# Block-sparse attention from the second batch on, with the drawn key blocks gathered by register offsets

## The chip, the cores and the metric

The kernel runs on one core of a Trainium2 chip. A core has five engines with instruction streams of their own: TensorE (PE, with its weight loads shown apart as PEld), VectorE (DVE), ScalarE (ACT), GpSimd (POOL) and SyncE (SP, which computes nothing and issues most DMAs here). They are tied together by semaphores, and each engine takes its instructions strictly in the order in which they were written. The metric is the device time of one execution in microseconds. Before the change it was 1061.06 us (median of 3 runs, 1060.33 to 1061.57).

## The reference

Attention over 4 batches, 8 heads, 768 positions of 64 numbers, with a block mask (24 blocks of 32), and then a Fourier mixing block with a two-layer channel network. All is float32.

```python
scores = scale * np.matmul(q, k.transpose(0, 1, 3, 2))
mask = np.abs(blk_i - blk_j) <= 1                       # neighbouring blocks
mask = mask | (blk_i == 0) | (blk_j == 0) | (blk_i == n_blocks - 1) | (blk_j == n_blocks - 1)
for qb in range(n_blocks):
    for kb in sampled_blocks[qb]:                       # three drawn blocks per query block
        mask[qb * block:(qb + 1) * block, kb * block:(kb + 1) * block] = True
scores = np.where(mask, scores, -1000000000.0)
attn = softmax(scores)                                  # max taken off, exp, divided by the sum + 1e-9
x = (attn @ v), heads side by side                      # (4, 768, 512)
mixed = np.real(np.fft.fft(np.fft.fft(x, axis=1), axis=2))
u = x + mixed
un = (u - mean(u)) / np.sqrt(var(u) + 1e-06)
return u + np.maximum(un @ w_ch1, 0.0) @ w_ch2          # 512 -> 2048 -> 512
```

A query block needs its own block, two neighbours, the first, the last and up to three drawn ones: at most 8 of 24. The queries of the first and the last block need every key. The drawn blocks are an input, known only when the kernel runs.

## The kernel before

**Pairs and units.** Two heads of one batch make a *pair*, 16 pairs in all (`pairs`, four to a batch). The two heads lie on the two halves of the 128 partitions. A pair has 12 *units* (`UP`): two halves of the queries (384 each) by six chunks of 128 keys. For a unit, `scores` (L560) makes 128 x 384 scores of each head in PSUM (L577, each head on its 64 rows of the array); `weigh` (L591) takes the exponential on ACT; `values` (L641) multiplies with v and adds into `o` over the six chunks (L651); `gather` (L618) adds the exponentials on POOL or DVE, for the sums of the softmax. All keys are computed, and the mask takes out what doesn't belong: either PE adds large negative numbers from two small factor tables (L587, while `masks["by_pe"]` holds), or DVE multiplies by a 0/1 mask after the exponential (L607; the mask is made in the first batch by `mask_step`, L367).

**Queries and keys.** For the first five pairs PE transposes q and k (`turn`, L495). From then on (`BY_VECTOR`) `load_blocks` (L221) loads 32x32 blocks with four transfers each for q and k, and DVE flips the blocks (`flip_blocks`). The queries stand in an order of their own (`_ORDER`) which the Fourier part wants; `in_order` copies q into it.

**Output.** When a half is done, `values` copies `o` to `oT` and `place` (PE) or `place_blocks` (L685: 16 transfers from SBUF to SBUF, issued on SP, in batches 2 and 3 for all but a batch's first pair) brings it into `x`, the tile of the batch. `x` has two buffers a half, so the third batch can be placed only when the first has left.

**The order of the work.** All instructions are in an order written out at build time. `slot` (L1379) takes two units at a time, 6 slots a pair, 24 a batch: scores of this slot, values of the one before, loads of later pairs, placing. Between, it puts the work of the batch before: the Fourier steps (`apart`) as gaps allow, and the channel products (`late`; `quad`, L1053 and `channels`, L1118) at a pace. The gaps come from a planner's own estimates of each engine's time (`when`, `busy`). At the first pair of the third and fourth batch, `until` (L1433, L1449) runs the channel products of the batch two back to the end as one block, since its `x` is needed. The channel weights are loaded and rounded beside the first batch's attention (`w_load`, `w_round`).

**Queues.** Nearly every DMA is issued on SP, in program order: q, k and v two pairs or one pair ahead, tables and weights in the first batch, `place_blocks`, the output. If SP has to wait for a buffer, everything behind it waits too.

Of the kernel before, what the change touches and what calls it, by code (L numbers as in the profile page):

```python
# [40 lines left out]
def _grid(ap, start, runs, jump, n, step):  # L41
# [25 lines left out]
_IN_ORDER = ((0, 0, (128, 128, 2), (64, 1, 2), (1, 2, 64)),  # L67
# [32 lines left out]
def kernel(  # L100
# [68 lines left out]
    mask = const.tile([P, C, S], U8, name="mask")  # L169
# [4 lines left out]
    ldv = ctx.enter_context(tc.tile_pool(name="ldv", bufs=2))  # L174
# [44 lines left out]
    BY_VECTOR = NP + 1  # L219

    def load_blocks(n, a, tile):  # L221


        b, j = pairs[n]
        for i in range(2):
            rows = (q, k)[a][b, 2 * j + i].rearrange("(t r) (g d) -> g r t d", r=BLK, d=BLK)
            for g in range(D // BLK):
                p0 = D * i + BLK * g
                nc.sync.dma_start(
                    out=tile[p0:p0 + BLK, :].rearrange("r (t d) -> r t d", d=BLK), in_=rows[g])  # L230
        loaded[n, a] = tile

    def load_k(n, queue=None, cuts=(slice(0, C),)):

        if n >= BY_VECTOR:
            load_blocks(n, 1, ld.tile([P, S], FP32, tag="k", name="kb"))
            return
# [11 lines left out]
    def load_q(n, ts=range(T)):  # L249

        if n >= BY_VECTOR:
            load_blocks(n, 0, ld.tile([P, S], FP32, tag="q", name="qb"))
            return
# [10 lines left out]
    def load_v(n, queue=None):  # L264

        b, j = pairs[n]
        vt = ldv.tile([P, 2, C, D], FP32, tag="v", name="vr")
# [3 lines left out]
        v_of[n] = vt  # L271

# [64 lines left out]
    factors = room(2, [P, 3, S], "factors", BF16)  # L337
    of_k, off_q, keep_q = (factors[:, i, :] for i in range(3))
# [3 lines left out]
    nc.vector.memset(keep_q, 0.0)  # L342

    def twice(t):
# [17 lines left out]
    keep = bit(NB)  # L362
    nc.vector.tensor_scalar(out=keep, in0=maskT, scalar1=0.0, scalar2=None,
                            op0=ALU.is_equal)
    spread_q(off_q[0:NB, :], maskT)
    twice(off_q)
    def mask_step(i):  # L367


        half, c = divmod(i, C)  # L370
        m, at = ps_m.tile([P, 512], FP32, tag="m", name="m"), bank("m")
        nc.tensor.matmul(m[:, 0:HS], of_k[0:D, c * P:(c + 1) * P],
                         keep_q[0:D, half * HS:(half + 1) * HS], start=True, stop=True)
        done = busy("PE", 0.17) + HOP

        def keep_it():
            nc.scalar.copy(out=mask[:, c, half * HS:(half + 1) * HS], in_=m[:, 0:HS])
            give(at, busy("ACT", 0.5, done))
        return keep_it
# [106 lines left out]
    by_pe, to_gather = set(), deque()  # L486
    masks = {"by_pe": True}

    turned, e_of, acc_of, o_of, sums_of, x_of, sp_of = {}, {}, {}, {}, {}, {}, {}
    s_at, e_at, e_free, oT_at, acc_at = {}, {}, {}, {}, {}  # L490
# [38 lines left out]
    def squares(n, a):  # L529

        t = loaded[n, a]
        if a == 0:
            turned[n, 0] = tp_p.tile([P, S], FP32, tag="qT", name="qT")
        nc.scalar.activation(out=t if a else turned[n, 0], in_=t, func=ACT.Square,
                             accum_out=peaks[:, 2 * n + a:2 * n + a + 1])
        busy("ACT", 1.05)

    def flip_blocks(n, a):
        t = loaded[n, a]
        out = t  # L540
        if a == 1:
            kT = turned[n, 1] = tp_p.tile([P, S], FP32, tag="kT", name="kT")
            out = _at(kT, 0, [(1, P), (P, C)])
        nc.vector.transpose(out=out, in_=t)
        busy("DVE", 1.0)

    def in_order(n):

        t = loaded[n, 0]
        qT = turned[n, 0]  # L550
        for to, frm, *dims in _IN_ORDER:
# [66 lines left out]
    def gather(u):  # L618
# [4 lines left out]
        if c == 0:  # L623
            return
# [1021 lines left out]
```

## Time and profile before

| what | value |
|---|---|
| median of 3 runs | 1061.06 us |
| the profiled execution | 1061.69 us, its span 1060.0 us |
| granted TensorE clock, mean | 0.994 |
| PE / DVE / ACT / POOL busy | 97% / 63% / 35% / 23% of the span |
| attention of pairs 0 to 3 (batch 0) | 7.8 to 126.8 us |
| pairs 4 to 7 (batch 1) | to 229 us |
| scores of pair 8, then the block of batch 0's channel products | to 248, to 410 us |
| pairs 9 to 11 with channel products between | to 537 us |
| pair 12, then a block of channel products | to 556, to 657 us |
| pairs 13 to 15 with channel products between | to 778 us |
| the rest: channel products, Fourier part and channel network of batch 3 | to 1060 us |

The page shows one profiled execution. Busy shares are of the span; a float32 product appears as two PE records, each with a weight load of its own. In a line of groups, `x768 | 154.8, 518 | 7.4` reads: 768 instructions, 154.8 us busy together, 518 ns one of them, 7.4 us idle of the engine just before them. `SPq` is SP issuing a DMA: the time stands for the issue, not for the transfer.

### The profile page before, as it was taken

How to read it: one execution, taken by the hardware profiler on the slowest of the kernel's cores; microseconds unless marked ns; L12 is line 12 of the kernel's file. 1: busy time of each engine (PE TensorE's matmuls, PEld its weight loads, DVE VectorE, ACT ScalarE, POOL GpSimd, SP SyncE). 2: the span in 40 equal slices, each digit the busy share in tenths (PEclk: the TensorE clock that was granted, in tenths of full speed). 3: DMA queues.
4: the chain of work that ended last, by engine and by line, in shares of the span. 5: the costliest groups of instructions: out<-in, count | busy, mean ns of one | idle time of the engine just before them, and what ended most of it. 6: DMA issues, size and time to landing. Idle time of an engine off the chain costs nothing.

```text
span 1060.0 us, 12495 instructions
## 1 busy us (share of the span) xinstructions
PE 1030.6 (97%) x4414; PEld 537.1 (51%) x4414; DVE 669.1 (63%) x1227; ACT 366.5 (35%) x736; POOL 240.5 (23%) x270
## 2 busy tenths in 40 slices
PE   8989999999999999999999999899999999999996
PEld 4333345445465454443534654354445564578585
DVE  6898795877746345655678364765447446774663
ACT  6978755564020122433441212343221111210210
POOL 1000183556000002554552001635420001000000
PEclk9999999999999999999999999999999999999998
DMA  7757522220000002231220001210000001000001
GB/s 217 229 166 222 112 46 45 45 46 15 1 1 0 1 1 57 52 56 27 41 54 0 1 1 44 63 33 19 8 15 0 1 0 42 19 1 1 0 18 46
DMA packets 120544, 46.27 MB, mean 44 GB/s; under 512 B 108172, under 2 KB 113562, under 8 KB 120474
## 3 DMA queue, kind: packets, MB, share of 16 engines
q1 hardware_dynamic: 119222, 44.66, 17.6%
q10 hardware_dynamic: 1220, 0.72, 0.3%
q8 instruction: 36, 0.59, 0.2%
q14 instruction: 34, 0.28, 0.1%
q0 software_dynamic: 32, 0.01, 0.0%
HBM read 36.72 MB, written 6.29 MB: 41 GB/s over the span
## 4 chain that ended last, share of the span: by engine, by line
PE 87%; DVE 6%; ACT 4%; issue 2%; DMA 1%; SPq 0%; POOL 0%; ACTq 0%; DVEq 0%; POOLq 0%
PE y L1122 23%; PE z L1066 16%; PE s L577 11%; PE o L651 10%; PE yp L1066 8%; PE yy L1187 7%; PE xp L1066 4%; PE zp L855 2%; PE s L587 1%; DVE t L1028 1%; ACT e L597 1%; PE sp L718 1%; PE sp L732 1%; PE utp L991 1%; PE xt L674 1%
## 5 line engine op out<-in xcount | busy, mean ns | idle before, releaser
L637 POOL TENSOR_TENSOR acc<-acc,e 128x384 f32<-128x384 f32 x158 | 160.9, 1052 | 87.1 <-DVE e L607 68.0
L577 PE MATMUL s<-qT,kT 64*128 64x384 f32 x768 | 154.8, 518 | 7.4 <-ACT e L597 5.8
L651 PE MATMUL o<-e,vr 128*64 128x384 f32 x768 | 143.1, 500 | 2.2 <-DVE oT L659 2.2
L1125 DVE TENSOR_TENSOR x<-y,x 128x512 f32<-128x512 f32 x72 | 49.8, 691 | 130.1 <-PE y L1122 129.8
L1122 PE MATMUL y<-w_sb,hB 128*128 128x512 f32 x288 | 128.0, 595 | 0.3 <-DVE x L1125 0.3
L1122 PE MATMUL y<-w_sb,hA 128*128 128x512 f32 x288 | 128.1, 594 | 0.0
L607 DVE TENSOR_TENSOR e<-s,mask 128x768 f32<-128x768 f32 x88 | 80.0, 950 | 48.9 <-ACT s L605 39.9
L577 PEld LDWEIGHTS s<-qT,kT 64*128 64x128 f32 x768 | 64.5, 187 | 85.7 <-ACT e L597 23.6
L605 ACT ACTIVATE s<-s 128x768 f32<-128x768 f32 x88 | 66.7, 792 | 92.6 <-PE s L577 92.4
L637 POOL TENSOR_TENSOR acc<-e 128x384 f32<-128x384 f32 x46 | 50.3, 1113 | 212.0 <-ACT e L597 125.9
L597 ACT ACTIVATE e<-s 128x768 f32<-128x768 f32 x104 | 79.1, 810 | 49.0 <-PE s L587 36.4
L1066 PE MATMUL z<-unT,t 128*128 128x384 f32 x256 | 93.4, 487 | 0.6 <-DVE hA L1071 0.6
L1122 PEld LDWEIGHTS y<-w_sb,hB 128*128 128x128 f32 x288 | 53.5, 190 | 65.5 <-issue 64.6
L1122 PEld LDWEIGHTS y<-w_sb,hA 128*128 128x128 f32 x288 | 53.6, 190 | 62.6 <-issue 59.9
L651 PEld LDWEIGHTS o<-e,vr 128*64 128x64 f32 x768 | 48.0, 136 | 72.7 <-issue 67.8
L1071 DVE TENSOR_TENSOR hA<-z,hA 128x384 f32<-128x384 f32 x64 | 35.7, 557 | 70.6 <-PE z L1066 70.6
L1075 ACT ACTIVATE hA<-hA 128x384 f32<-128x384 f32 x64 | 33.6, 524 | 122.5 <-DVE hA L1071 122.4
L1066 PEld LDWEIGHTS z<-unT,t 128*128 128x128 f32 x256 | 48.2, 190 | 35.6 <-DVE hA L1071 3.0
L1075 ACT ACTIVATE hB<-hB 128x384 f32<-128x384 f32 x64 | 33.6, 525 | 86.0 <-DVE hB L1071 86.0
L938 POOL TENSOR_SCALAR st<-st 128x1 f32<-128x1 f32 x24 | 8.3, 347 | 207.4 <-DVE st L937 207.3
L1086 ACT COPY hA<-xp 128x384 f32<-128x384 f32 x32 | 15.3, 479 | 111.6 <-PE xp L1066 111.6
L1066 PE MATMUL z<-t,w_sb 128*128 128x384 f32 x128 | 46.7, 488 | 0.7 <-DVE t L1028 0.7
(207 smaller groups left out, 1430.7 us busy)
## 6 DMA issues: line engine op xcount, KB each, us to landing
wraw<-in_moe_w_ch_dram SPq DMA_DIRECT2D x32, 512.0 KB
vr<-in_v_dram SPq DMA_DIRECT2D x30, 192.0 KB
qb<-in_q_dram SPq DMA_DIRECT2D x44, 96.0 KB
kb<-in_k_dram SPq DMA_DIRECT2D x44, 96.0 KB
x<-oT SPq DMA_DIRECT2D x192, 12.0 KB
out_dram<-x SPq DMA_DIRECT2D x11, 252.0 KB
out_dram<-x SPq DMA_DIRECT2D x18, 128.0 KB
qr<-in_q_dram SPq DMA_DIRECT2D x24, 64.0 KB
```

What stands on the lines that cost most here:

```text
L577: nc.tensor.matmul(s[:, i, 0:HS], kT[rows, c * P:(c + 1) * P], qT[rows, queries], start=True, stop=u not in by_pe)
L597: nc.scalar.activation(out=e, in_=s[:, :, 0:HS], func=ACT.Exp, scale=scale)
L605: nc.scalar.activation(out=s[:, :, 0:HS], in_=s[:, :, 0:HS], func=ACT.Exp, scale=scale)
L607: nc.vector.tensor_tensor(out=e, in0=s[:, :, 0:HS], in1=m.broadcast_to([P, 2, HS]), op=ALU.mult)
L637: nc.gpsimd.tensor_add(out=acc[:, i, :], in0=start[:, i, :], in1=e[:, i, :])
L651: nc.tensor.matmul(o[D * i:D * i + D, :], vt[:, i, c, :], e[:, i, :], start=(c == 0), stop=(c == C - 1))
L1066: nc.tensor.matmul(to, a[:, k, :], c[:, k, :], start=(k == 0), stop=(k == ND // 2 - 1))
L1071: tt(out=to, in0=ps, in1=a, op=ALU.add)
L1075: nc.scalar.activation(out=h, in_=h, func=ACT.Relu)
L1122: nc.tensor.matmul(y, hs[0, half][:, l, m * P:(m + 1) * P], w2_sb[:, 4 * r + l, :], start=(l == 0), stop=(l == 3))
L1125: nc.vector.tensor_tensor(out=x[:, m, :], in0=y, in1=x[:, m, :], op=ALU.add)
L1187: nc.tensor.matmul(ps, a[:, k, :], c[k // 2][:, k % 2, :] if isinstance(c, list) else c[:, k, :], start=(k == 0), stop=(k == 3))
```

## The change

For pairs 4 to 15 attention no longer computes all keys. A pair has 8 units in place of 12, in 4 slots (`KINDS`), and each half of the queries has four kinds:

- **E** and **O**: windows. The keys lie in eight chunks of three blocks (96 keys), with the first or the last block of all appended to each chunk by `copy_ends`, so that 128 keys meet the queries near them (`_WINDOWS`). Together they cover neighbours, the first and the last block. 352 query columns each; a table `near` of 0 and 1 takes out what doubles.
- **X**: drawn. For each of the 11 inner query blocks of the half, three drawn key blocks side by side (96 keys) meet 32 queries: 11 pieces. `gather_drawn` copies the key blocks on POOL from the flipped keys to `kr`, 33 copies of 32 columns at offsets read from a table into POOL's registers. `load_drawn` brings the same blocks of v from DRAM, 33 transfers on SP with an offset in a register. A table `drawn` takes out blocks that are drawn twice or are covered by a window.
- **G**: the queries of the first and the last block, against all keys: four chunks of 96 keys, 64 columns.

Score products are cut to 64 keys, so that one product covers a 64x64 part of the array. `kr` is one buffer for both halves. The drawn values lie in two tiles of the pool `ld`, which has one buffer for each name; both halves use the same two. q and k are loaded straight into the tiles that are flipped in place (k in 12 transfers a pair, before 4), v in chunks with the first and last block behind them (12 transfers a pair, before 2). The order of the queries is now made when `o` is copied out (`put`, small copies on ACT) and, for the sums, in `invert` (small copies on DVE). The tables are made once, in the first batch (`near_masks`, `drawn_load`, `drawn_masks`); `mask_step` and the mask are gone. Pair 4 is no longer transposed by PE.

Core of the diff:

```diff
-    BY_VECTOR = NP + 1
+    BY_VECTOR = NP
...
+                for x in range(CH):
+                    nc.sync.dma_start(
+                        out=tile[p0:p0 + BLK, :, BLK * x:BLK * x + BLK],
+                        in_=of.rearrange("(c x r) (g d) -> x g r c d", x=CH, r=BLK, d=BLK)[x, g])
...
+    def drawn_at(engine, row, most, m):
+        return nc.values_load_multi_w_load_instructions(
+            at_of[row:row + 1, NR * m:NR * min(m + 6, NQ)], engines=[engine], min_val=0, max_val=most,
+            skip_runtime_bounds_check_because="kept within the blocks by a minimum on the chip")[1]
...
+    def load_drawn(n, half):
+        b, j = pairs[n]
+        vr_of[n, half] = [ld.tile([P, 6, 2, D], FP32, tag=tag, name="vd") for tag in "qk"]
+        for m in range(NQ):
+            if m % 6 == 0:
+                at = drawn_at(mybir.EngineType.SP, 2 * BLK + BLK * half, S - BLK, m)
+            for r in range(NR):
+                nc.sync.dma_start(
+                    out=vr_of[n, half][m // 6][BLK * r:BLK * r + BLK, m % 6, :, :],
+                    in_=v[b, 2 * j:2 * j + 2, bass.ds(at[NR * (m % 6) + r], BLK), :].rearrange(
+                        "h s d -> s h d"))
+
+    def gather_drawn(n, half):
+        flat = turned[n, 1].rearrange("p c s -> p (c s)")
+        for m in range(NQ):
+            if m % 6 == 0:
+                at = drawn_at(mybir.EngineType.Pool, BLK * half, NCH * P - 2 * BLK, m)
+            for r in range(NR):
+                nc.gpsimd.tensor_copy(out=kr[:, m, BLK * r:BLK * r + BLK],
+                                      in_=flat[:, bass.ds(at[NR * (m % 6) + r], BLK)])
...
+    KINDS = ((0, "E"), (0, "O"), (0, "X"), (0, "G"), (1, "G"), (1, "E"), (1, "O"), (1, "X"))
...
+            for keys, to, of in parts:                      # few_scores
+                for i in range(2):
+                    for g in range(0, keys.shape[1], D):
+                        rows = slice(D * i, D * i + D)
+                        some = keys[rows, g:min(g + D, keys.shape[1])]
+                        nc.tensor.matmul(s[g:g + some.shape[1], i, to], some, of[rows],
+                                         start=True, stop=True)
...
+        elif kind == "X":                                   # few_values
+            rows = slice(0, NR * BLK)
+            parts = [(vr_of[n, half][m // 6][:, m % 6], to, to, False, True)
+                     for m, to, _ in pieces(half, kind)]
...
+        for vals, to, of, start, stop in parts:
+            for i in range(2):
+                nc.tensor.matmul(o[D * i:D * i + D, to], vals[rows, i, :], e[rows, i, of],
+                                 start=start, stop=stop, skip_group_check=True)
...
     def slot(sl):
...
+        if NP <= nxt < len(pairs):
+            if s == 0:
+                load_k(nxt)
+                load_q(nxt)
+            if s == (4 if not few else 2):
+                for a in (1, 0):
+                    squares(nxt, a)
+                    flip_blocks(nxt, a)
+                copy_ends(nxt)
+            if s == (5 if not few else 3):
+                gather_drawn(nxt, 0)
+            if s == 1:
+                load_chunks(nxt, 0)
+        if few and s == 1:
+            gather_drawn(n, 1)
+        if NP <= n < len(pairs) and s == 0:
+            load_chunks(n, 1)
+            load_drawn(n, 0)
+        if few and s == 2:
+            load_drawn(n, 1)
```

Scores of a slot come before the values of the slot before. So X of half 0 has its scores in slot 1 and its values in slot 2; X of half 1 has its scores in slot 3 and its values in slot 0 of the next pair.

More of the change, by code (lines that the diff above doesn't have):

```diff
@@ new lines, in gather_drawn @@
+    def gather_drawn(n, half):
[6 more added lines that the diff above has]
+                                      in_=flat[:, bass.ds(at[NR * (m % 6) + r], BLK)])
+                busy("POOL", 0.2)
+        kr_at[n, half] = when["POOL"] + HOP
@@ L538, in flip_blocks @@
     def flip_blocks(n, a):
[L539 to L544, printed above, removed]
-        busy("DVE", 1.0)
[L547 to L551, printed above, removed]
-            nc.scalar.copy(out=_at(qT, to, [(d[0], d[2]) for d in dims]),
-                           in_=_at(t, frm, [(d[1], d[2]) for d in dims]))
-        busy("ACT", 1.7, when["DVE"])
+        t = turned[n, a][:, :, 0:CH * BLK] if a else turned[n, 0]
@@ L556, with copy_ends @@
+        nc.vector.transpose(out=t, in_=t)
+        busy("DVE", 1.0)
+    def copy_ends(n):
+        kT = turned[n, 1]
+        last = CH * BLK
+        for odd, (c, x) in enumerate(((0, 0), (NCH - 1, CH - 1))):
+            src = kT[:, c, BLK * x:BLK * x + BLK].rearrange("p (o r) -> p o r", o=1)
+            nc.scalar.copy(out=kT[:, odd::2, last:last + BLK],
+                           in_=src.broadcast_to([P, NCH // 2, BLK]))
+        busy("ACT", 0.6, when["DVE"] + HOP)
     UP = 2 * C
-    UNITS = len(pairs) * UP
@@ L657, in values @@
             oT = sum_p.tile([P, HS], FP32, tag="oT", name="oT")
[L658 to L663 removed]
+            nc.scalar.copy(out=oT, in_=o_of.pop((n, half)))
+            oT_at[n, half] = busy("ACT", 0.5, when["PE"] + HOP) + HOP
             o_of[n, half] = oT
```

539 lines of the change are left out of this document (370 added, 169 removed), and 7 rows, old and new, of tables (_IN_ORDER, _PLACED).

## The prediction

> **What bounds the kernel now.** I read the page's shares, then the sliced page and the windows by stage, then the costliest groups, and last the two views that a small transfer shows in: the timeline of SP, and the answers for the lines that issue on it.
>
> ```profile
> PE 1030.6 (97%) x4414; PEld 537.1 (51%) x4414; DVE 669.1 (63%) x1227; ACT 366.5 (35%) x736; POOL 240.5 (23%) x270
> ...
> PE 87%; DVE 6%; ACT 4%; issue 2%; DMA 1%; SPq 0%; POOL 0%; ACTq 0%; DVEq 0%; POOLq 0%
> ...
> L577 PE MATMUL s<-qT,kT 64*128 64x384 f32 x768 | 154.8, 518 | 7.4 <-ACT e L597 5.8
> ...
> L651 PE MATMUL o<-e,vr 128*64 128x384 f32 x768 | 143.1, 500 | 2.2 <-DVE oT L659 2.2
> ```
>
> TensorE is busy 97% and holds 87% of the chain that ended last. A float32 product stands as two records, so the 768 records of L577 are 384 products: all 16 pairs times 12 units times two heads. The windows by stage (columns: PE, PEld, DVE, ACT, POOL busy with instruction counts, clock, DMA share, GB/s) are the batch 1 pairs, the work beside pairs 9 to 11, beside pairs 13 to 15, and the tail:
>
> ```profile
> 126.80:229.00 102.20, 100.45 (x629) 47.16 (x627) 75.79 (x112) 59.72 (x124) 57.71 (x55) 1.00 0.26 49
> ...
> 410.00:537.00 127.00, 126.28 (x529) 56.77 (x528) 77.75 (x111) 50.85 (x98) 59.27 (x60) 1.00 0.24 46
> ...
> 657.00:778.00 121.00, 117.83 (x492) 52.02 (x490) 70.89 (x99) 43.70 (x79) 56.96 (x58) 0.99 0.16 31
> 778.00:1060.00 282.00, 268.52 (x957) 171.62 (x955) 160.45 (x326) 43.02 (x89) 8.90 (x17) 0.99 0.05 13
> ```
>
> So a batch 1 pair takes 25.6 us and a pair of the later groups of three 40 to 42 us, all with PE full. Now the timeline of SP (start, us, instruction), which holds no share of the chain today:
>
> ```profile
> 443.36 10.39 SPq L690 DMA_DIRECT2D x<-oT  x16
> ...
> 460.98 10.21 SPq L690 DMA_DIRECT2D x<-oT  x16
> ```
>
> The answers for the issuing lines (count: min/median/max ns, first and last start):
>
> ```profile
> L229 SPq DMA_DIRECT2D qb<-in_q_dram x44: 311/524/1952, 111.3 to 677.3; - x44
> ...
> L1538 POOLq TENSOR_LOAD <-flag x1: 487/487/487, 775.5 to 775.5; - x1
> L1538 SPq TENSOR_LOAD <-flag x1: 737/737/737, 781.6 to 781.6; - x1
> L1538 SPq FUSED_REGOPS  x1: 192/192/192, 782.4 to 782.4; - x1
> ```
>
> Sixteen transfers of 12 KB hold SP for 10.2 us, 0.64 each, with nothing to wait for: the price is in the issue. A 96 KB load costs 0.52 plus 0.045 to the next, 0.57, so bytes hardly matter; the first of a burst costs 0.31. A value read into a register costs SP 0.80 from start to start, and address arithmetic 0.19.
>
> **The change part by part.** *PE, removed.* By the timeline, scores of two units run 1.49 us and values of four 2.73, 1.43 a unit: 17.1 a pair. Also gone are the mask products of the 56 later units that have them (25.9/104 = 0.25 each, 14 in all), the mask steps (3.9) and the PE transposes of pair 4 (1.3).
>
> *PE, added.* A record streams a column in 0.84 ns (12 records of 384 columns in 3.87 us). E and O have 352 columns each, twice 0.59 us a half; G 256, 0.43. X has 11 pieces of 32 columns, so weight loads set its pace: loads last 136 ns for 64 columns and 190 for 128, 0.85 ns a column, hence 54 for 64, twice per piece, 1.2 us if the tiles of the array overlap as the heads of L577 do. Scores and values of both halves are four times 2.8, 11.3, and 0.8 for the breaks between groups: 12.1 a pair. If the tiles of X did not overlap, at the 0.11 of a 128-column transpose (four run from 409.32 to 409.76 in PE's timeline) 88 records would make the scores of X 9.7 us, 44 its values 4.8, and a pair 36. PE then gains 12 x 5.0 + 19 = 79 us, or loses 211.
>
> *SP, added.* Each half gathers drawn values with 33 transfers, 66 a pair: 32 rows by two heads by 256 bytes. The two nearest rows are 0.57 (32 partitions, from HBM) and 0.64 (96 runs); I take 0.64. The register arithmetic (0.235 with its gap) falls in time that SP now spends between 0.31 and 0.57, so I add nothing; ends 0.36 (no such waiting) and 0.88 (nothing overlaps). Register loads come in groups of 18 and 15. If a group is one load it costs 0.80; if each value is a load, 14.4 and 12.0. No row decides; I take the middle in ratio, 3.4 and 3.1, and keep 1.6 and 26.4 a half as ends. [...] K goes from 4 transfers to 12 and v from 2 to 12; with q that is 28 at 0.57, 16.0 a pair. In batches 2 and 3, pairs with j > 0 keep 32 placing transfers at 0.64, 20.5.
>
> *Why this is on the path.* The tiles of drawn values are single: SP can issue half 1 only when X of half 0 has been multiplied, and the next pair's half 0 only after X of half 1. PE runs in the written order, so it stands at X until the 33 transfers are in, with some 6 us of its own work between. K, q, v and placing transfers queue on the same SP, behind or ahead. A pair therefore takes SP's time: 66 x 0.64 = 42.2, loads 13.0, others 16.0, and about 1 us a half for a landing (the one row that has it, 2.8, partly overlapped): 73 us, or 94 with placing, against 25.6 and 40 to 42. PE's 79 us of savings are swallowed in these waits.
>
> *POOL.* Leaves the 11 sums of each half for 66 register-addressed copies: 0.35 (nearest row, 128x1) plus 0.235 is 39 a pair, loads 13, adds about 10: 62, under SP's 73. At the 0.67 of its slower 128x1 row and one load per value, 106.
>
> *DVE and ACT.* DVE: six masks of 704 columns at 0.87, two flips at 1.0, sums: about 10 us; ACT: eight exponentials and a dozen small copies, 11 us; both behind SP's 73, and still behind PE if SP were free. After the last pair the order copies of sums and of the output cost some 4 us uncovered. The new masks in the first batch are some 30 small DVE instructions, balanced by the mask copies removed: nothing, at most 4.
>
> *The sum, along the profiled execution (span 1060.0, 1061.7 with what lies around it; median of the runs 1061.1).* Pair 3's last scores, near 121, free the buffer for pair 5's k. From there SP issues 16 loads (9.1), six of v (3.4), then pair 4's first half (21.1 + 6.5), landing 2.8: X at 164. Four pairs at 73 bring X of pair 8 to 457. Four us later the block of channel products that now runs from 248 to 410 follows, 162: 623. Pair 9's first half, 34: 657. Three pairs at 73 and five placings at 10.2: 927. Pair 12 and its block (556 to 657, 101): 1032. Pair 13's lead 34, two pairs, three placings: 1243. The last placing and half, 41: 1284. The tail of 282 and 4: 1570, that is my time (the 1.7 around the span is lost in the rounding).
>
> **The rivals.** *One load per value* (same mechanism): a pair 113, the same walk 2008. The multi-value call speaks against it, the lack of any multi-register row for it. *SP issues without waiting*, 0.36 and 0.80 a group: a pair 45, the walk 1260; some overlap ahead of need would take it to 1180. Every full burst above speaks against it. *POOL is the bound*: 106 us in place of 73 and 94, 1785; X scores would be late, not X values. *Faster:* the gathers are hidden and PE stays the bound: 1060 - 79 = 981. This needs 94 transfers and the loads inside PE's 17.6 us of a batch 1 pair (25.6 less 5.0 and twelve mask products), under 0.19 us a transfer; the cheapest issue on SP, of one row, is 0.22. [...]
>
> **How the numbers follow.** Group loads near the middle, 1570: 0.54, its own range 1400 to 1700. One load per value, 2008: 0.24. Cheap issue, 1180 to 1260: 0.08. POOL, 1785: 0.08. Faster, 981: 0.05. The remaining 0.01 is no change: within 0.2%, about what a measurement tells from none. Leaving the fast case and the far ends out, the range is 1180 to 2050; faster 0.05, same 0.01, slower 0.94.
>
> **What would show it.** Right: SP's lines for drawn values near 0.64 each, 33 in a row, and PE's X products waiting for those transfers, about 70 us from one X of half 0 to the next in batch 1, the windows of batch 1 with PE half idle, the block and tail lengths as before. Wrong: PE over 90% busy in batch 1, X scores waiting for POOL's copies, or X itself taking 5 us or more of PE.

## The result and the profile after

The changed kernel takes 1507.2 us (median of four executions, 1504.4 to 1511.5) against 1061.3 (1060.3 to 1062.8): a ratio of 1.420, with a 95% interval of 1.416 to 1.424. It is slower by 446 us; the forecast was 1570, with a range of 1180 to 2050. The profiled execution took 1506.4, its span 1504.7.

From the page of the changed kernel: the busy shares of the engines, the granted clock of TensorE in 40 slices (tenths of full speed), and the chain that ended last by engine and by line.

```profile
PE 1311.6 (87%) x8886; PEld 838.4 (56%) x8886; DVE 638.7 (42%) x1275; ACT 324.5 (22%) x733; POOL 248.4 (17%) x991
...
PEclk9998667567879998676765579986766789999999
...
PE 58%; SPq 26%; issue 6%; DMA 4%; DVE 3%; ACT 2%; POOL 1%; POOLq 0%; DVEq 0%; ACTq 0%
...
PE y L1392 14%; SPq L336 13%; PE s L734 13%; PE z L1336 10%; SPq L950 5%; PE yp L1336 5%; PE yy L1460 5%; SPq L322 4%; PE xp L1336 3%; PE o L835 3%; PE zp L1125 1%; SPq L253 1%; PE s L889 1%; DMA out_dram<-x 1%; SPq L316 1%
```

PE's share fell from 97% to 87%, and SP's sequencer, which held nothing of the chain, now holds 26%. L336 is the transfer of drawn values, L950 the placing of outputs, L322 the register loads. The clock, close to 1.0 throughout before, is at 5 to 8 tenths in three stretches. The two groups of PE that belong to drawn blocks, X scores and X values (busy us, mean ns, then idle time before them and what ended it):

```profile
L734 PE MATMUL s<-qT,kr 64*64 64x32 f32 (+1 forms) x2112 | 288.9, 261 | 1.8 <-POOL kr L348 0.9
...
L835 PE MATMUL o<-e,vd 96*64 96x32 f32 x1056 | 51.3, 234 | 81.8 <-DMA vd<-in_v_dram 81.8
```

The X scores are PE's largest single group, 288.9 us for 24 halves, 12 us each; PE stood only 1.8 us in all ahead of them. The X values take 51.3, and PE stood 81.8 us for their transfers. SP's timeline (start, us, instruction), from half 1 of pair 4, the first pair of batch 1, to half 1 of pair 5:

```profile
163.89 21.22 SPq L336 DMA_DIRECT2D vd<-in_v_dram  x33
...
199.07 20.68 SPq L336 DMA_DIRECT2D vd<-in_v_dram  x33
...
225.05 21.28 SPq L336 DMA_DIRECT2D vd<-in_v_dram  x33
```

A half starts at 163.89, 199.07 and 225.05, and a pair, from 163.89 to 225.05, lasts 61 us. Two bursts of 33 transfers, the loads of k and q for the next pair (5.7 and 3.2 us), of v, and of registers fill it almost without a break. PE's timeline beside it, half 0 of pair 5:

```profile
187.54 12.98 PE L734 MATMUL s<-qT,kr 64*64 64x32 f32 x88
...
215.07 0.31 PE L835 MATMUL o<-e,vd 96*64 96x32 f32 x4 [1.81 <-DMA vd<-in_v_dram]
216.53 0.31 PE L835 MATMUL o<-e,vd 96*64 96x32 f32 x4 [1.16 <-DMA vd<-in_v_dram]
```

First the X scores for 13 us; then the X values arrive piece by piece, and PE waits more than a microsecond for each group of four records (two products: one piece for two heads, from three transfers). A window over the pairs of batch 1, with the columns as before (the granted clock is the third number from the right):

```profile
127.00:400.00 273.00, 231.28 (x2323) 172.96 (x2316) 103.53 (x186) 60.95 (x148) 72.12 (x325) 0.69 0.22 41
```

The tail takes 278 us from the last X values at 1226.6 to the end, where it took 282 before; the whole difference lies ahead of it.

### The profile page after: what moved, and what is told of

The parts are those of the page before. It is cut to its first block, busy times and chain, and to the rows that moved or that the text cites. A ratio compares the mean times of both kernels' runs of the same rounds, so it can differ in the third digit from the quotient of the medians.

```text
span 1504.7 us, 26093 instructions
## 1 busy us (share of the span) xinstructions
PE 1311.6 (87%) x8886; PEld 838.4 (56%) x8886; DVE 638.7 (42%) x1275; ACT 324.5 (22%) x733; POOL 248.4 (17%) x991
## 4 chain that ended last, share of the span: by engine, by line
PE 58%; SPq 26%; issue 6%; DMA 4%; DVE 3%; ACT 2%; POOL 1%; POOLq 0%; DVEq 0%; ACTq 0%
PE y L1392 14%; SPq L336 13%; PE s L734 13%; PE z L1336 10%; SPq L950 5%; PE yp L1336 5%; PE yy L1460 5%; SPq L322 4%; PE xp L1336 3%; PE o L835 3%; PE zp L1125 1%; SPq L253 1%; PE s L889 1%; DMA out_dram<-x 1%; SPq L316 1%
## 5 line engine op out<-in xcount | busy, mean ns | idle before, releaser
L734 PE MATMUL s<-qT,kr 64*64 64x32 f32 (+1 forms) x2112 | 288.9, 261 | 1.8 <-POOL kr L348 0.9
L734 PEld LDWEIGHTS s<-qT,kr 64*64 64x64 f32 (+1 forms) x2112 | 226.3, 156 | 66.3 <-issue 2.5
L348 POOL COPY kr<-kT 128x32 f32 x792 | 140.0, 229 | 173.6 <-ACT kT L677 64.9
L835 PE MATMUL o<-e,vd 96*64 96x32 f32 x1056 | 51.3, 234 | 81.8 <-DMA vd<-in_v_dram 81.8
L755 DVE TENSOR_TENSOR e<-s,near 128x704 f32<-128x704 f32 x48 | 41.8, 888 | 123.2 <-ACT s L751 121.8
L835 PEld LDWEIGHTS o<-e,vd 96*64 96x64 f32 x1056 | 44.4, 149 | 89.0 <-issue 64.1
L734 PE MATMUL s<-qT,kT 64*64 64x64 f32 (+6 forms) x1728 | 68.6, 314 | 18.5 <-ACT e L746 14.2
L751 ACT ACTIVATE s<-s 128x704 f32<-128x704 f32 (+1 forms) x72 | 51.3, 736 | 148.1 <-PE s L734 148.1
L734 PEld LDWEIGHTS s<-qT,kT 64*64 64x64 f32 x1728 | 51.7, 172 | 35.4 <-ACT e L746 14.5
L835 PE MATMUL o<-e,vv 96*64 96x64 f32 (+7 forms) x864 | 70.3, 326 | 1.1 <-ACT oT L846 1.1
```

The lines of the kernel that those rows point to most:

```text
L348: nc.gpsimd.tensor_copy(out=kr[:, m, BLK * r:BLK * r + BLK], in_=flat[:, bass.ds(at[NR * (m % 6) + r], BLK)])
L734: nc.tensor.matmul(s[g:g + some.shape[1], i, to], some, of[rows], start=True, stop=True)
L751: nc.scalar.activation(out=s[rows, :, cols], in_=s[rows, :, cols], func=ACT.Exp, scale=scale)
L755: nc.vector.tensor_tensor(out=e[rows, :, cols].rearrange("p i (m x) -> p i m x", x=BLK), in0=s[rows, :, cols].rearrange("p i (m x) -> p i ...
L835: nc.tensor.matmul(o[D * i:D * i + D, to], vals[rows, i, :], e[rows, i, of], start=start, stop=stop, skip_group_check=True)
```

## The experiments

All times below are medians of four executions, and the ratios are against the kernel before on the same chip. Each is an edit of the changed kernel, or of the kernel named.

**The order of the X products.** Within X every piece multiplies 64 drawn keys and then 32, so the tile on TensorE changes shape from product to product. The edit does all 64-key products first:

```diff
-            for keys, to, of in parts:
-                for i in range(2):
-                    for g in range(0, keys.shape[1], D):
+            for first in ((0, D) if kind == "X" else (None,)):
+              for keys, to, of in parts:
+                for i in range(2):
+                    for g in range(0, keys.shape[1], D) if first is None else (first,):
```

> Only the order of the X score products is changed: first all 64-key products of the 11 pieces, then all 32-key products, in place of changing between the two in every piece. In the trace of the changed kernel the scores of one X take 12.9 us, where the forecast had 1.2. Theory S (SP's issue of the drawn values sets the pace of every pair): X falls to about 2 us, but the first drawn-value transfers of half 1 still stand 61 us apart in batch 1 and about 83 us apart in the pairs with placing; the time stays between 1460 and 1510 us. Theory P (the scores of X set the pace): 24 halves lose about 11 us each, the time falls to about 1250 us. Third, that the products are slow whatever their order: X stays above 10 us and the time at 1507.

Measured: 1476.3 us, ratio 1.388 (1.385 to 1.391). The groups of X scores and X values:

```profile
L735 PE MATMUL s<-qT,kr 64*64 64x32 f32 (+1 forms) x2112 | 74.3, 237 | 0.8 <-POOL acc L787 0.5
...
L836 PE MATMUL o<-e,vd 96*64 96x32 f32 x1056 | 69.0, 252 | 176.5 <-DMA vd<-in_v_dram 176.5
```

X scores fall from 288.9 us to 74.3, by 215 us of PE time, and the kernel gains 31. The other 184 are not saved. PE's wait for the drawn values grows from 81.8 to 176.5 us, and its waits for other things with it. A pair of batch 1 still takes 61 us. SP sets the pace, and PE's slow X scores were hidden behind it. What is behind these 12 us is seen in windows over single halves (second column from the start: us, PE busy; third from the right: granted clock). The X scores of one half in the changed kernel, and of two halves with the order changed:

```profile
188.00:200.00 12.00, 12.00 (x84) 9.38 (x84) 5.28 (x12) 0.00 (x0) 5.91 (x29) 0.50 0.47 79
```

```profile
188.50:192.40 3.90, 3.90 (x96) 3.72 (x92) 3.62 (x7) 0.00 (x0) 1.59 (x5) 0.50 0.34 54
227.70:230.00 2.30, 2.30 (x102) 2.22 (x96) 2.23 (x9) 0.00 (x0) 0.23 (x1) 1.00 0.15 33
```

At a clock of 0.50, 13 us become 3.9; at 1.00 the ordered products take 2.3. Of the 44 alternating steps of a half (11 pieces, two heads, two widths) 43 change the shape, against one in the new order, so a change costs (12.98 - 3.87)/42 = 0.22 us at the halved clock. The new order also puts every product on the other head's rows than the one before it, but that is not the reason. The one change of shape that is left goes to the other head's rows too, and by the start times in the trace it takes 0.149 us at full clock and 0.221 at half (medians of 12 each), as the changes to 32 keys within one head's rows took in the old order; steps of 64 keys to the other head's rows without a change take 0.052 and 0.094. The traces show that a change takes time, and not what the array does in it.

**The transfers of drawn values.** Four transfers from fixed places for each half in place of 33, and no register loads on SP; the tile is filled as before.

```diff
-        for m in range(NQ):
-            if m % 6 == 0:
-                at = drawn_at(mybir.EngineType.SP, 2 * BLK + BLK * half, S - BLK, m)
-            for r in range(NR):
+        for t, first, cnt in ((0, 0, 6), (1, 1, 5)):
+            for i in range(2):
                 nc.sync.dma_start(
-                    out=vr_of[n, half][m // 6][BLK * r:BLK * r + BLK, m % 6, :, :],
-                    in_=v[b, 2 * j:2 * j + 2, bass.ds(at[NR * (m % 6) + r], BLK), :].rearrange(
-                        "h s d -> s h d"))
+                    out=vr_of[n, half][t][0:NR * BLK, 0:cnt, i, :],
+                    in_=v[b, 2 * j + i, NR * BLK * first:NR * BLK * (first + cnt), :].rearrange(
+                        "(m p) d -> p m d", p=NR * BLK))
```

> Leaves out the drawn choice of the values: each half loads blocks at fixed places, the same bytes in runs of the same 256 bytes, in 4 transfers in place of 33, without register loads (so the output is not the reference's). Everything else stays, the 12.9 us of X scores too. Theory S: a pair falls to what PE needs with the slow X, some 46 us in batch 1 (2 x 12.9 and 18 of other work, and breaks) and about 60 in the later groups; the time falls to 1230 to 1320 us. Theory P: within 30 us of 1507.

Measured: 1333.7 us, ratio 1.256 (1.253 to 1.259), 14 us above the expected range. SP leaves the chain (1%), and PE takes its place: busy 95%, with the line of all the new attention's scores at 25% of the chain; the X scores are busy 277.6 us. Here, with no wait for transfers in the way, the clock can be watched: windows over the 6 us before a group of X scores, and over the group.

```profile
301.50:307.50 6.00, 6.00 (x41) 3.45 (x40) 4.98 (x11) 1.67 (x4) 0.00 (x0) 1.00 0.00 1
307.50:319.30 11.80, 11.80 (x94) 9.26 (x92) 1.19 (x3) 0.42 (x1) 0.00 (x0) 0.61 0.22 35
```

PE was busy for all of the 6 us ahead, at a clock of 1.00; over the X scores the clock averages 0.61, though the records show PE busy there too. In 11 of the 24 halves it stands so, without any idle time before, and no half has its X scores above 0.74. The alternating shapes do not only cost their changes; the clock falls while they run, in these 11 halves 2.0 to 4.9 us after the first product.

**Both together.**

> Both: X score products grouped by width, and values from fixed places in 4 transfers (the drawn choice of values is left out). Theory S with PE as the next bound: 980 to 1040 us, the clock back at 0.95 or more. If the key copies on POOL are the next bound (8 to 11 us a half with their register loads, and each half has to wait for the other's scores, since there is one buffer): batch 1 pairs stay at 28 us or more and the time comes to 1040 to 1120 us. Theory P: no better than the run with grouped products alone.

Measured: 1142.3 us, ratio 1.074 (1.072 to 1.077), 22 us above the upper of the two ranges; theory P is out. From the page of this kernel, the busy shares:

```profile
PE 1032.4 (90%) x8886; PEld 637.3 (56%) x8886; DVE 638.0 (56%) x1275; ACT 324.2 (28%) x733; POOL 267.3 (23%) x991
```

Taken alone, the order of X is worth 31 us and the transfers 174; together they are worth 365. Each edit alone meets the other cost as the next bound: 61 us of SP a pair against some 47 us of PE. What is new is in the line shown: PE is busy 1032 us, where the kernel before stood at 1030.6, although the X scores, now in order, run at a clock of 1.00 in most halves. The saving of 79 us of PE that the forecast counted is not there.

**A buffer for each half.** The forecast gave as a reason that the tiles of drawn values are single. Here each half has its own; to fit, a transfer brings one head's values and both heads use them.

```diff
-        vr_of[n, half] = [ld.tile([P, 6, 2, D], FP32, tag=tag, name="vd") for tag in "qk"]
+        vr_of[n, half] = ld.tile([P, 2 * 6, 1, D], FP32, tag="qk"[half], name="vd")
...
-                    out=vr_of[n, half][m // 6][BLK * r:BLK * r + BLK, m % 6, :, :],
-                    in_=v[b, 2 * j:2 * j + 2, bass.ds(at[NR * (m % 6) + r], BLK), :].rearrange(
+                    out=vr_of[n, half][BLK * r:BLK * r + BLK, m, :, :],
+                    in_=v[b, 2 * j:2 * j + 1, bass.ds(at[NR * (m % 6) + r], BLK), :].rearrange(
```

> The edit, on the changed kernel: the drawn values of each half have a buffer of their own, so SP can issue half 1 while PE has yet to multiply half 0. For the room each transfer brings the values of one head, 8 KB instead of 16, which serve for both heads; the drawn values of the second head are left out of the result. The number of transfers and register loads is the same. In the changed kernel SP is at work for some 57 of the 61 us of a batch 1 pair. Theory S (the issue on SP sets the pace, whatever the buffers): the 33 transfers keep their 0.51 us each, the pair falls only by the 4 us of gap, 1440 to 1510. Theory H (the hand-over of the one buffer sets it: SP waits for PE and PE for SP in turn): SP's and PE's work overlap and the pair falls well below 50 us, under 1400.

Measured: 1503.9 us, ratio 1.414 (1.411 to 1.418), the time of the changed kernel. SP's bursts of the first pair:

```profile
165.49 21.07 SPq L336 DMA_DIRECT2D vd<-in_v_dram  x33
...
226.83 20.91 SPq L336 DMA_DIRECT2D vd<-in_v_dram  x33
```

The bursts are as long with 8 KB a transfer as with 16, and a pair is 61 us, as before. The single buffer costs nothing that a second would give back: SP's own instructions fill the pair.

**Fixed places, the same 33 transfers.** This splits the price of a transfer from that of its register address.

```diff
-            if m % 6 == 0:
-                at = drawn_at(mybir.EngineType.SP, 2 * BLK + BLK * half, S - BLK, m)
             for r in range(NR):
...
-                    in_=v[b, 2 * j:2 * j + 2, bass.ds(at[NR * (m % 6) + r], BLK), :].rearrange(
+                    in_=v[b, 2 * j:2 * j + 2, BLK * ((7 * m + 5 * r) % NB):BLK * ((7 * m + 5 * r) % NB) + BLK, :].rearrange(
```

> The edit, on the changed kernel: the 33 transfers of drawn values of each half stay, each of the same size, but from fixed places, without register loads and address arithmetic on SP; the drawn choice of values is left out of the result. In the changed kernel a half holds SP 22.5 us: loads of 1.4 and 3.1 us and 33 transfers at a pitch of 0.51, of which the arithmetic and the move stand for 0.08 and more. Theory S1 (the pitch of a transfer is its own, the arithmetic falls in its waiting): the pitch stays at 0.48 to 0.55, only the loads go, 24 halves x 4.5 = 108 us: 1390 to 1420. Theory S2 (the arithmetic is paid in full): the pitch falls to 0.32 to 0.40, another 24 x 33 x 0.15 = 119 us: 1270 to 1310.

Measured: 1405.8 us, ratio 1.323 (1.319 to 1.326). One burst on SP:

```profile
156.71 16.39 SPq L334 DMA_DIRECT2D vd<-in_v_dram  x33
```

That is 16.39/33 = 0.50 us a transfer over the whole burst; start to start the median is 0.470 us, against 0.507 with registers. The issue is the price, and address arithmetic adds 0.04 to it, 1.2 us a half. The pitch lies a hair under S1's range and far from S2's. The 101 us gained are mostly the register loads. A pair of batch 1 takes 49 us; PE alone needs 47 in the kernel with four transfers, so the gain stops there in any case.

**The second register load.** It reads 15 values and takes 3.07 us, where the first reads 18 in 1.4. The edit lengthens the second to 18 by three zeros.

```diff
-    at_of = const.tile([P, NQ * NR], I32, name="at_of")
+    at_of = const.tile([P, (NQ + 1) * NR], I32, name="at_of")
...
-            at_of[row:row + 1, NR * m:NR * min(m + 6, NQ)], engines=[engine], min_val=0, max_val=most,
+            at_of[row:row + 1, NR * m:NR * (m + 6)], engines=[engine], min_val=0, max_val=most,
...
+        nc.vector.memset(at_of, 0)
```

> The edit, on the changed kernel: the second register load of each half reads 18 values, as the first does, instead of 15 (the list is padded by three zeros). In the changed kernel the load of 18 values took 1.40 us on SP, and the second, of 15, 3.07. If the cost hangs on the number of values (15 is read in more steps than 18): both take about 1.4 us, a half on SP shrinks by 1.67 us, and 24 halves give 40 us: 1460 to 1475. If it hangs on the place (the second load, or its start within the list): the second load stays near 3 us and the time at 1500 to 1512.

Measured: 1519.4 us (1515.2 to 1524.5), ratio 1.431 (1.427 to 1.436): 12 us slower than the changed kernel, and outside both expected ranges, since the second load grew. The answer for the loads, in the changed kernel and with 18 and 18 (min, median and max ns):

```profile
L322 SPq TENSOR_LOAD <-at_of x48: 1385/2975/3088, 136.5 to 1206.6; - x48
```

```profile
L322 SPq TENSOR_LOAD <-at_of x48: 1387/3250/3690, 137.5 to 1217.8; - x48
```

The second load goes from 3.07 to 3.67 us, in all 24 halves: 0.205 and 0.204 us a value. The first stays at 1.39 to 1.62 in 22 of 24, 0.08 a value. The cost hangs on the place and then on the number. In the last kernel below, the two kinds of load are issued more than 20 us apart. By its SP timelines, the gap between issues that holds a load from the list's start is 1.64 to 1.93 us, the one that holds the other 3.32 to 3.64 (four of each): so it is the place in the list, not that one load follows another. Why, the runs do not show.

**No gather of keys either.** From the kernel with both edits, POOL's register loads and its 66 copies a pair are taken out, and X multiplies fixed columns of kT:

```diff
-        flat = turned[n, 1].rearrange("p c s -> p (c s)")
-        for m in range(NQ):
-            if m % 6 == 0:
-                at = drawn_at(mybir.EngineType.Pool, BLK * half, NCH * P - 2 * BLK, m)
-            for r in range(NR):
-                nc.gpsimd.tensor_copy(out=kr[:, m, BLK * r:BLK * r + BLK],
-                                      in_=flat[:, bass.ds(at[NR * (m % 6) + r], BLK)])
-                busy("POOL", 0.2)
...
-                parts = [(kr[:, m, :], to, qT[:, of]) for m, to, of in pieces(half, kind)]
+                parts = [(kT[:, m % NCH, 0:NR * BLK], to, qT[:, of]) for m, to, of in pieces(half, kind)]
```

> The edit: as the kernel with both edits (grouped X products, four fixed transfers of values per half), and besides the gather of drawn keys is left out: no register loads and no copies on POOL, the X scores multiply fixed columns of kT. So the drawn choice of keys and values is left out of the result. With both edits a batch 1 pair took 35 us (26 before the change), PE stood at 30 of these 35 with a granted clock of 0.85, and the copies on POOL (7.7 us of span a half, one buffer kr for both halves) stood between the X scores of one half and the next. Theory G (what is left is held by the key gather on POOL and its one buffer): the pair falls to about 28 us, 12 pairs give 12 x 7 = 84 us, 1040 to 1085, and PE's granted clock in batch 1 comes back above 0.93. Theory W (PE's own work in the new attention is no smaller than in the old, many small products, so taking the gather away moves little): 1105 to 1145, the pair stays above 32 us.

Measured: 1128.6 us, ratio 1.061 (1.058 to 1.064). Nearly W: POOL's busy time falls from 267 to 111 us, the kernel gains 14, and PE's busy time stays at 1032.5. From X of pair 4 to X of pair 7 a pair takes 31.0 us, where the kernel with both edits has 31.8 by the same count (the 35 of the expectation was counted on later halves). PE is still not full, and waits are left. One of them, traced from SP through ACT and DVE to PE (timelines of four engines, one line or two of each; brackets: idle time before, and what ended it):

```profile
555.14 12.12 SPq L940 DMA_DIRECT2D x<-oT  x16
...
568.73 0.86 ACT L836 COPY oT<-o 128x32 f32<-128x32 f32 x6 [9.24 <-DMA x<-oT]
...
569.62 0.58 DVE L858 STREAM_TRANSPOSE oT<-oT 128x384 f32<-128x384 f32 x1 [8.53 <-DMA kT<-in_k_dram]
...
574.13 0.87 PE L1005 MATMUL st<-ident,sums 128*128 128x128 f32 x3 [8.05 <-DVE sums L999]
```

Twelve us of placing on SP free the buffer of a half's output; ACT's copy into that buffer stood 9.2 us for it; DVE's flip of it follows (the profile names the key transfer as the releaser, but ACT's copies to the same tile end just ahead of the flip); and PE stood 8.1 us for the sums behind that. ACT's waits of this kind add up to 51.6 us in this kernel.

**Outputs placed by TensorE.** One line: every half goes the way that the first pairs go, through a transpose on PE.

```diff
-        return n > 2 * NP and n % NP > 0
+        return False
```

On the kernel without any gather:

> The edit: as the kernel that gathers neither drawn values nor drawn keys (1129 us; the drawn choice of both is left out of the result), and besides no output half is flipped and placed by 16 transfers on SP; TensorE transposes and places all of them, as it does for the first pair of a batch. That takes 192 transfers of 0.64 us, 123 us, off SP in the second and third batch, and gives TensorE 36 transposes and ACT 12 copies. In the 1129 us kernel a K load (567 to 575) stood on SP behind 12 us of placing, DVE stood at the flip of that K, and PE stood 8.0 us for DVE's sums and 11.7 us for DVE's hA, which waited for placed x. Theory Q (in the groups beside the channel products, what is left is this queue of K loads behind placings): PE's waits for sums and hA go, 1075 to 1105. Theory W (PE's own work in the new attention, at a lower granted clock, is what is left): 1110 to 1130.

Measured: 1089.5 us, ratio 1.024 (1.022 to 1.027). Q's time, but perhaps not Q's mechanism: in the one wait traced above, what stood behind the placings was the output buffer and not the K load. The edit takes both away, so this run does not tell them apart. Busy shares, PE's two largest waits (us in total, times, longest), then the windows of batch 1 and of a stretch beside the channel products:

```profile
PE 1017.2 (93%) x8922; PEld 630.3 (58%) x8922; DVE 634.3 (58%) x1263; ACT 329.1 (30%) x745; POOL 111.0 (10%) x199
```

```profile
PE s L724 <- DVE e L745: 14.2, 10, 3.9
PE s L724 <- ACT e L736: 11.4, 2, 7.9
```

```profile
127.00:254.00 127.00, 109.91 (x2081) 84.34 (x2077) 95.28 (x173) 54.89 (x135) 11.58 (x26) 0.87 0.41 79
740.00:795.00 55.00, 55.00 (x757) 35.39 (x754) 21.77 (x35) 16.09 (x42) 13.73 (x18) 1.00 0.17 36
```

With no gather, no placing and one shape after another, it is still 27 us above the kernel before. PE is busy 13 us less than there, but it waits longer: its scores stand 14.2 us for DVE's masks and 11.4 for ACT's exponentials, where they stood 1.5 and 5.8 before. In batch 1 the clock stays at 0.87; beside the channel products it is 1.00. There one whole pair can be added up at full clock. PE's timeline (two value groups, 0.66 and 0.69 us, are left out):

```profile
757.64 1.49 PE L724 MATMUL s<-qT,kT 64*64 64x128 f32 x40
759.05 1.43 PE L825 MATMUL o<-e,vv 128*64 128x160 f32 x20
760.31 1.43 PE L825 MATMUL o<-e,vd 96*64 96x32 f32 x44
...
761.86 2.91 PE L724 MATMUL s<-qT,kT 64*64 64x32 f32 x120
...
779.90 1.29 PE L724 MATMUL s<-qT,kT 64*64 64x64 f32 x48
781.12 1.48 PE L825 MATMUL o<-e,vv 128*64 128x128 f32 x20
782.43 1.43 PE L825 MATMUL o<-e,vd 96*64 96x32 f32 x44
784.28 2.90 PE L724 MATMUL s<-qT,kT 64*64 64x64 f32 x112
```

The four score groups are 1.49 + 2.91 + 1.29 + 2.90 = 8.6 us, the values 1.43 + 1.43 + 1.48 + 1.43 + 0.66 + 0.69 = 7.1: 15.7 a pair.

On the kernel that does the whole computation and has the ordered X:

> The edit: the whole computation, as the kernel with grouped X products (1476 us), and besides TensorE places all output halves; no placing transfers on SP. Theory S (SP's issue sets the pace of every pair from batch 1 on): the pairs of batches 2 and 3 lose 20.5 us of SP's time, 84 becomes about 63, 6 pairs with placing give 123 us: 1340 to 1375. If the placing lies in time in which SP waits anyhow (for X's values or for tiles), the time falls by less than 60 us: above 1416.

Measured: 1366.9 us, ratio 1.286 (1.284 to 1.289), 109 us less than with ordered X alone (which ran on another chip; its ratio of 1.388 says the same). The three pairs of batch 2 with placing, from X of pair 9 to X of pair 12, fall from 262 us to 189, or 63 a pair, about what a pair of batch 1 takes. S holds: most of the 123 us of placing was on the path.

**The drawn values of a batch set apart once.** The drawn places are the same for all heads. So one register-addressed transfer can take a block for all eight heads, into a buffer in HBM; each pair then takes its two heads from fixed places. This does the whole computation, with both edits above:

```diff
+    def set_apart(b, half, m0):
+        n = min(6, NQ - m0)
+        to = apart_of[b, half, m0] = dr_p.tile([NR * BLK, n, H, D], FP32,
+                                               tag="a%d%d%d" % (b, half, m0), name="ap")
+        at = drawn_at(mybir.EngineType.SP, 2 * BLK + BLK * half, S - BLK, m0)
+        for m in range(n):
+            for r in range(NR):
+                nc.sync.dma_start(
+                    out=to[BLK * r:BLK * r + BLK, m, :, :],
+                    in_=v[b, :, bass.ds(at[NR * m + r], BLK), :].rearrange("h s d -> s h d"))
...
+        for m0 in (0, 6):                                   # load_drawn
+            cnt = min(6, NQ - m0)
+            nc.sync.dma_start(out=vr_of[n, half][m0 // 6][0:NR * BLK, 0:cnt, :, :],
+                              in_=apart_of[b, half, m0][:, :, 2 * j:2 * j + 2, :])
...
+            if phase + 1 < B:                               # slot 2 of a pair
+                set_apart(phase + 1, (n % NP) // 2, 6 * (n % 2))
+        if sl in (12, 15, 18, 21):                          # batch 0
+            set_apart(1, (sl - 12) // 6, 6 * (sl // 3 % 2))
```

> The edit: the whole computation, as the kernel with grouped X products and all halves placed by TensorE (1367 us), but the drawn value blocks of all eight heads of a batch are fetched once, by 66 register-addressed transfers of 64 KB into a buffer in HBM, one group of 18 or 15 a pair, a batch ahead; each half then takes them by two transfers from fixed places. SP's register-addressed transfers fall from 792 to 198. Theory S (SP's count of instructions, not its bytes, is the price): a pair's SP time falls from 57 to 16 (loads) + 12 (one group) + 2, under PE's; the time comes near the kernel that gathers nothing and places by TensorE (1090), plus the 14 us that the key gather was worth: 1095 to 1150. If the transfers by way of HBM cost by their bytes (17 MB more read and written), above 1200. Either way it stays above the kernel before, since PE's own work in the new attention was no smaller.

Measured: 1197.5 us (1196.2 to 1202.1), ratio 1.129 (1.126 to 1.132): 169 us less than without it, but 47 above the upper end of what S expected, and 3 below where its rival, a cost by bytes, begins. By the time alone it stands between the two. SP holds 7% of the chain. Where the rest lies is seen by the times of the X values beside those of the kernel without any gather: the first X of batch 1 ends at 188.9 in place of 147.1, 42 us later; four pairs on it is 65 later, at the last X 105. The groups for batch 1 stand on SP in batch 0, and PE waits there (timelines of SP and PE):

```profile
80.97 13.40 SPq L337 DMA_DIRECT2D ap<-in_v_dram  x18
...
104.89 11.61 SPq L337 DMA_DIRECT2D ap<-in_v_dram  x15
...
152.35 0.90 PE L944 MATMUL xt<-ident,oT 128*128 128x128 f32 x3 [14.23 <-ACT oT L932]
```

A transfer of 64 KB takes 13.40/18 = 0.74 us on SP, not 0.51: four times the bytes cost half as much again. With its register load a group holds SP for 15 us, ahead of the loads of batch 0. By the page, 13 MB more are read from HBM and 13 more written, not the 17 of the expectation. PE's wait of 14.2 us for ACT's output copy is the largest wait there; the runs don't follow it back to one transfer. The rest of the gap, 63 us, holds the key gather (14 by the comparison above) and what was not taken apart. This kernel does not beat the kernel before. The kernel without any gather stands at 1090, so a better way of gathering alone is not likely to either, as long as the attention's products, masks and their order stay as they are.

## Why the prediction was right, and where its steps were off

**SP as the bound: right.** The chain, SP's full bursts, and PE's waits are the ones that the forecast described. Undoing only the transfers gives 174 us, only the order of X 31, and both 365.

**The price of SP's steps: each somewhat too high.** A transfer was put at 0.64 and measured 0.507, a half's register loads at 6.5 and measured 4.5. A half holds SP 22.5 us, not 27.6, and a batch 1 pair 61 us, not 73. Where placings add to it, three pairs of batch 2 took 262 us, close to the 270 of the walk, and two of batch 3 149, not 177. The walk along the kernel kept its shape: X of pair 4 at 161 (forecast 164), of pair 8 at 409 (457), the block of channel products 150 us (162), pair 15's half 0 at 1191 (1243), its half 1 at 1226.6 (1284). The last sum is 57 us too high there, and the tail of 278 in place of 282 and 4 gives the rest of the 63 us between 1570 and 1507. The 0.64 was the row of the placing transfers, which take that here too: 10.2 to 11.7 us for 16, 0.64 from start to start in the median. Of the two nearest rows, the other, 0.57, was nearer. That arithmetic would fall into SP's waiting was nearly right: it costs 0.04 a transfer, taken as nothing.

**One load or many values: not decided, and near by luck.** A group is one instruction, so the rival of one load per value, 2008 us, was not there. But the forecast had no row that told which, and took the middle in ratio between the two, 3.4 and 3.1 us. The loads take 1.4 and 3.07. That the middle came near is luck; the forecast gave this case 0.54.

**The single tiles as the reason: wrong, without effect.** A tile of its own for each half changes the pair by nothing measurable. SP is filled by its own instructions; it has no time to run ahead.

**The X scores: outside both bounds.** They were put at 1.2 us a half, at most 9.7, and take 10.4 to 13.0. The step took the tiles as overlapping, or as separate at the price of a 128-column transpose. Neither counts the change of shape between 64 and 32 keys, nor the halved clock. Ordered, they take 2.3 at full clock, still twice the 1.2. X values, 1.43, were nearly right. The miss was hidden in the total because SP's 61 us a pair covered PE; without SP's price it would have been the bound, at 47 us a pair. That it did not show in the time is luck too. The forecast had named it as a sign of being wrong (X itself taking 5 us or more of PE), and this sign came; and of its signs of being right one did not: PE is not half idle in batch 1 but busy for 231 of 273 us. That SP still set the pace is shown by the experiments, not by these signs. With the transfers made cheap and nothing else changed, the time was 1334 us, far from the rivals that the forecast worked out for cheap issue, 1180 to 1260 and 981.

**PE's gain of 79 us: wrong.** At full clock a pair costs 15.7 us, not 12.1. By the forecast's own count of what goes (12 x 17.1 + 19.2 = 224), that leaves 36 us, not 79. Of these 13 are seen: PE is busy 1017 us with nothing gathered and all outputs placed by PE. Of the other 23, PE's added transposes are 6 (their line goes from 11.1 to 17.4 us); the rest fits the lower clock, 0.96 in the mean in place of 0.99, which no run sets apart. So the "faster" rival's 981 was no price of cheap gathers: with all gathers free the kernel stands at 1129, and with the outputs placed by PE too at 1090. The chance of 0.05 could have been lower.

**The placings: right.** They went onto the path, and taking them off SP gave 109 of 123 us.

**POOL, DVE and ACT behind SP: right for the changed kernel.** POOL, busy 248 us, has 1% of the chain. The key gather is worth 14 us only when the values' transfers and X's order no longer cover it. That DVE and ACT would stay behind PE if SP were free did not hold: with nothing gathered and nothing placed by SP, PE waits more for their masks and exponentials than before, by the two lines shown.

## What to carry to other kernels

Count a gather in instructions on the queue that issues it: here 66 small transfers a pair at half a microsecond each cost more than the dense products that they replaced, and 33 of 8 KB took as long as 33 of 16, 21 us. Work saved on TensorE by cutting products into narrow pieces must be priced at the pieces' own rate and at the clock that is granted while they run, and products of one tile shape should be put side by side: at a clock of 0.50 that took the X scores of a half from 13 us to 3.9. When two engines are both near the bound, undoing one cost alone shows little: here 31 and 174 us singly, 365 together.

## What the runs showed of the hardware

The granted clock of TensorE differed by kernel and by stretch. In the kernel before it was 0.99 to 1.00 in the four stretches shown; in the changed kernel it averages 0.69 over the pairs of batch 1 and stands at 0.50 in 12 of the 24 groups of X scores, with PE shown busy throughout. With nothing gathered it is still 0.87 in batch 1. Idle time of PE does not stand ahead of every fall: in the changed kernel the clock falls 36 times, while PE has 18 gaps of more than 2 us; ahead of 9 of the falls PE is shown busy for all of 6 us. In the kernel with four transfers the clock fell from 1.00 within runs of products that show no gap, in the 6 us before or in them. With those products in order (the kernel with both edits) most of these groups ran at 1.00, but they are over in 2.3 us, and the clock fell 2.0 to 4.9 us into the others. So the clock falls while PE is shown busy on these small alternating products. Whether the change of shape or the small products lower it, and why, the runs leave open.

A register load on SP cost 0.08 us a value from the start of the list and 0.20 from 72 bytes into it. A change between tiles of 64 and 32 columns cost 0.22 us at the halved clock.
